# Attention, routing and two expert layers on one core: wider units of q and k, and an earlier place for the store of a group's rows

## The chip, the cores and the metric

The kernel runs on one core of a Trainium2 chip (trn2). The core has five engines that run their own instruction queues: TensorE (PE; its weight loads are shown apart as PEld), VectorE (DVE), ScalarE (ACT), GpSimd (POOL) and SyncE (SP, which here only issues DMAs). The metric is the device time of one execution, in microseconds (us); times of kernels are medians of several executions, and one further execution of each was recorded by the hardware profiler.

## The reference

```python
# q, k, v: [8 batches, 8 heads, 576 tokens, 64]; attention within chunks of 64 tokens
scores = (q_c @ k_c.T) / 8;  attn = softmax(scores);  x = (attn @ v_c) as [4608 tokens, 512]

# first expert layer: tokens with x @ w_skip > 0 go to one of 8 experts
e = argmax(x @ w_gate);  g = softmax(x @ w_gate)[e]
x[chosen] += g * (relu(x @ w1[e]) @ w2[e])          # w1 512x1024, w2 1024x512

# second layer, dense
h = max(relu(x @ w1'), x @ w2', x @ w3');  out = h @ w_out   # 512x768, 768x512
```

All of it is in 32-bit floats. The large products are made of three products of split operands (a high and a low part).

## The kernel before

The kernel has three stages. The first, the only one that the diff touches, makes attention and routing for 36 tiles of 128 tokens; the second runs the experts over gathered rows; the third is the dense layer in blocks of 1024 tokens.

**The loop of the first stage** (line 578) has one step t for each tile, and a tile passes through it over several steps. In step t: `cross(t)` (line 210) copies halves of the tile's v to the other 64 partitions (POOL, tile vm, four buffers); `pair_heads` (218) regroups q and k of a later unit (POOL, tiles qr and kr, three buffers); `values(t - 2)` (278) multiplies attention by v and writes the rows xg (DVE, line 300); `load_v` brings v of tile t + 6; `scores(t)` (244) makes q k, maximum, difference and exponential; `exp_transpose(t - 1)`; `logits(t - 3)`; `qk_transpose` (226) turns regrouped q and k, 4 transposes each on PE (tiles trq, trk, line 237), and ACT copies them out (line 239); `x_transpose(t - 2)` turns the rows (trx, line 313). PE's order is the written one (`manual_schedule`, 577). The other engines' queues are ordered by the scheduler of the build, from the written order and its own estimate of times, so an instruction may stand ahead of its written place or behind it.

**Units.** q and k come in 18 units of 256 tokens (UT). A partition holds two consecutive tokens (r=2), so for each head a packet of a load is 2 x 64 floats, 512 bytes. `load_qk` (190) issues q and k on SP, in two pieces each where a unit lies in two batches; five units have buffers (tags b4, s4, b8 of bpool), and a unit's load waits until the regroup of the fifth unit before has read the buffer. Unit u + 1 is turned in steps 2u and 2u + 1, four heads in each. The turned tiles qT and kT are 4 x 256 per partition with two buffers.

**Groups.** Routing runs over groups of four tiles (the last two groups have two). The step after a group's last logits has `route(g)` (324): some 20 small DVE instructions and an exponential; one of them, the reciprocal at line 343, writes the gate weight into the group's rows xg. A step later `place(g)` (378) makes ranks and slots, and `store_x(g)` (445) stores the group's rows to DRAM, 1 MB, issued by POOL. The rows of a group have two buffers (bpool tag xg), so the first rows of group g + 2 wait for the store of group g. `send_id(t - 9)` (425) scatters the 128 token numbers of a tile to their slots in DRAM, an indirect DMA issued by POOL. After group 5, the ids come back from DRAM, and DVE and POOL prepare the first gathers of the experts (lines 630 to 638).

From step 22 on, weights of expert 0 are loaded and split in even steps into wpool (tag w, 16 buffers of 4 KB per partition, two for each of eight pieces).

Of the kernel before, what the change touches and what calls it, by code (L numbers as in the profile page):

```python
# [28 lines left out]
NU = N // UT  # L29
# [8 lines left out]
def kernel(  # L38
# [151 lines left out]
    def load_qk(u):  # L190
        if u % 5 < 3:
            qt = four_kb([P, H, 2 * D], F32, f"qt{u}", u % 5 == 2)
            kt = four_kb([P, H, 2 * D], F32, f"kt{u}", u % 5 == 2)
        else:
            both = bpool.tile([P, 2, H, 2 * D], F32, tag="b8", name=f"qkt{u}")
            qt, kt = both[:, 0], both[:, 1]
        for h0, h1 in [(0, 4), (4, 8)] if u == 0 else [(0, 8)]:
            for off, b, s, n in pieces(u * UT, (u + 1) * UT):
                pr = slice(off // 2, (off + n) // 2)
                for dst, src in ((qt, q), (kt, k)):  # L200
                    link["load"] = nc.sync.dma_start(
                        dst[pr, h0:h1], src[b, h0:h1, s:s + n, :].rearrange("h (p r) d -> p h (r d)", r=2))
        units[u] = {"qt": qt, "kt": kt}
# [14 lines left out]
    def pair_heads(u, g):  # L218
        un = units[u]
        for nm in ("q", "k"):  # L220
            r = apool.tile([P, 2, H // 2, D], F32, tag=nm + "r", name=f"{nm}r{u}_{g}", bufs=3)
            (nc.scalar.copy if u == 0 else nc.gpsimd.tensor_copy if u > 1 else nc.vector.tensor_copy)(
                r, un[nm + "t"][:, 4 * g:4 * g + 4, :].rearrange("p h (r d) -> p r h d", r=2))
            un[nm + "r", g] = r

    def qk_transpose(u, g):
        un = units[u]
        if g == 0:
            for nm in ("qT", "kT"):
                un[nm] = apool.tile([P, 4, UT], F32, tag=nm, name=f"{nm}{u}")  # L230
        for nm in ("q", "k"):
            src, dst = un[nm + "r", g], un[nm + "T"]
            tr = ps_tr(f"tr{nm}{u}_{g}").rearrange("p (h r t) -> p h r t", h=2, r=2)
            for hh in range(2):
                hp = 2 * g + hh
# [3 lines left out]
            (nc.vector.tensor_copy if nm == "k" and u == 0 else nc.scalar.copy)(  # L239
                dst[:, 2 * g:2 * g + 2, :].rearrange("p h (t r) -> p h r t", r=2), tr)  # L240
# [3 lines left out]
    def scores(t):  # L244
        u, s = divmod(t, 2)
        un = units[u]
# [316 lines left out]
    for u in range(5):  # L563
# [5 lines left out]
        if u < 2:  # L569
            pair_heads(u, 0)  # L570
            pair_heads(u, 1)
            if u == 0:
                qk_transpose(0, 0)
                qk_transpose(0, 1)
# [555 lines left out]
```

## Time and profile before

| | |
|---|---|
| three runs | 1135.57, 1136.97, 1143.81 us; median 1136.97 |
| profiled execution | 1130.38 us; span from first to last instruction 1128.7; mean granted clock 0.952 |
| PE | 1032.5 us busy, 91% of the span |
| DVE, ACT, POOL | 570.0, 418.7, 363.8 us busy |
| loads of q and k, 512 KB | median 7.0 and 7.3 us from issue to landing (tiles qt, kt) |
| stores of a group's rows, 1040 KB | median 6.7 us |

How to read the rows: an engine's busy time is what its instructions fill; its waits are idle stretches, put down to the event that came last among those that the instruction waited for. Where a wait is for several events and one is an engine that updates all the time, the name shown can be that engine's though another event ended the wait. [...] A DMA share of 1.00 means that 16 engines' worth of packet time was used. A tile's name stands without its number.

### The profile page before, as it was taken

The page shows a single profiled execution, that of the slowest core. Times are in us where ns is not written, and L with a number is a line of the kernel's source. Part 1 is how long each engine was busy: PE and PEld are TensorE (multiplying, and loading weights), DVE is VectorE, ACT ScalarE, POOL GpSimd, SP SyncE. Part 2 cuts the span into 40 slices and gives each one's busy share as a digit, 9 for nine tenths or more (in the row PEclk, how much of TensorE's full clock was granted, in tenths as well). Part 3 has the DMA queues.
Part 4 walks back from the last instruction along what each step waited for, and adds up shares of the span by engine and source line. Part 5 has one row for each costly group of instructions (what it writes and reads, how often), then busy time and mean ns, then how long its engine had stood idle before and what let it go on. Part 6 is the DMA issues. An engine that isn't in the chain of part 4 may idle for free.

```text
span 1128.7 us, 19653 instructions
## 1 busy us (share of the span) xinstructions
PE 1032.5 (91%) x7544; PEld 879.0 (78%) x7544; DVE 570.0 (51%) x1118; ACT 418.7 (37%) x737; POOL 363.8 (32%) x411
## 2 busy tenths in 40 slices
PE   8967886897999997999899799999999999999997
PEld 6866875795887886888688588778887788788896
DVE  4653664646973646542479781444334352343241
ACT  5644554533543433451434352222322242222231
POOL 3445566344451335350332241111311140122121
PEclk9988788798999998999999899999999999999999
DMA  9999754446783728461998835665456644666590
GB/s 211 231 261 213 181 156 148 152 142 226 246 284 111 264 91 281 165 221 47 286 327 297 274 105 182 179 182 154 166 158 188 195 131 142 193 195 199 180 294 37
DMA packets 213105, 217.12 MB, mean 192 GB/s; under 512 B 48267, under 2 KB 177291, under 8 KB 212992
## 3 DMA queue, kind: packets, MB, share of 16 engines
q1 hardware_dynamic: 199808, 174.18, 53.2%
q0 software_dynamic: 10592, 33.20, 8.6%
q10 hardware_dynamic: 2592, 8.26, 1.9%
q8 instruction: 69, 1.13, 0.4%
q14 instruction: 44, 0.36, 0.1%
HBM read 175.15 MB, written 41.83 MB: 192 GB/s over the span
## 4 chain that ended last, share of the span: by engine, by line
PE 44%; DMA 5%; DVE 1%; issue 0%; ACT 0%; SPq 0%; ACTq 0%; DVEq 0%
PE f_a L687 6%; PE f_a L689 6%; PE f_a L688 6%; PE o L687 4%; PE o L689 4%; PE o L688 4%; DMA ws<-m_sums 4%; PE f_d L687 3%; PE f_d L688 3%; PE f_d L689 3%; PE f_b L689 1%; PE f_b L688 1%; PE f_b L687 1%; PE trf L861 1%; DMA m_sums<-n_q 1%
## 5 line engine op out<-in xcount | busy, mean ns | idle before, releaser
L91 POOL TENSOR_TENSOR fh<-best,fh 128x512 fp32r<-128x512 f32 (+1 forms) x60 | 77.0, 1288 | 360.3 <-ACT fh L90 276.1
L687 PE MATMUL f_a<-x_t,ws 128*128 128x512 f32 (+1 forms) x270 | 100.9, 374 | 6.8 <-DVE p L1015 5.5
L688 PE MATMUL f_a<-x_t,ws 128*128 128x512 f32 (+1 forms) x270 | 99.9, 370 | 0.0
L689 PE MATMUL f_a<-x_t,ws 128*128 128x512 f32 (+1 forms) x270 | 99.7, 370 | 0.0
L90 ACT CAST whi_e<-raw_e 128x1024 fp32r<-128x1024 f32 x64 | 65.9, 1048 | 65.2 <-DMA raw_e<-in_moe_w_dram 33.8
L687 PE MATMUL h<-xhi,whi_e 128*128 128x256 f32 x256 | 74.6, 292 | 13.2 <-ACTq L964 7.4
L688 PE MATMUL o<-wlo_m,fh 128*128 128x512 f32 x216 | 84.6, 392 | 0.0
L687 PE MATMUL o<-whi_m,fh 128*128 128x512 f32 x216 | 83.4, 392 | 0.0
L689 PE MATMUL o<-whi_m,fh 128*128 128x512 f32 x216 | 83.4, 392 | 0.0
L688 PE MATMUL h<-xlo,whi_e 128*128 128x256 f32 x256 | 73.8, 289 | 0.1
L687 PE MATMUL y<-whi_e,hhi 128*128 128x512 f32 x184 | 73.2, 400 | 0.6 <-ACT hhi L754 0.6
L689 PE MATMUL h<-xhi,wlo_e 128*128 128x256 f32 x256 | 73.4, 288 | 0.0
L689 PE MATMUL y<-whi_e,hlo 128*128 128x512 f32 x184 | 72.2, 396 | 0.2
L688 PE MATMUL y<-wlo_e,hhi 128*128 128x512 f32 x184 | 71.8, 392 | 0.0
L91 POOL TENSOR_TENSOR wlo_e<-raw_e,whi_e 128x1024 fp32r<-128x1024 f32 x21 | 52.8, 2516 | 51.2 <-ACT whi_e L90 50.9
L90 ACT CAST fh<-best 128x512 fp32r<-128x512 f32 (+1 forms) x60 | 34.8, 579 | 90.7 <-DVE best L1017 59.0
L91 DVE TENSOR_TENSOR wlo_e<-raw_e,whi_e 128x1024 fp32r<-128x1024 f32 x43 | 55.8, 1313 | 23.4 <-ACT whi_e L90 21.4
L687 PEld LDWEIGHTS f_a<-x_t,ws 128*128 128x128 f32 x270 | 51.1, 189 | 16.5 <-DVE p L1015 5.9
L687 PEld LDWEIGHTS h<-xhi,whi_e 128*128 128x128 f32 x256 | 50.4, 197 | 16.1 <-ACTq L964 10.8
L1020 ACT COPY p<-f_a 128x512 f32<-128x512 f32 (+1 forms) x45 | 24.6, 546 | 97.8 <-PE f_a L689 95.0
L678 POOL DMA_INDIRECT x_dram<-xg,ids_sb x20 | 20.8, 1039 | 115.3 <-DVEq L902 46.9
L689 PEld LDWEIGHTS f_a<-x_t,ws 128*128 128x128 f32 x270 | 51.2, 190 | 8.6
(220 smaller groups left out, 2709.5 us busy)
## 6 DMA issues: line engine op xcount, KB each, us to landing
ws<-m_sums SPq DMA_DIRECT2D x135, 512.0 KB, 5.0
raw_e<-in_moe_w_dram SPq DMA_DIRECT2D x64, 512.0 KB, 4.5
ws<-m_sums SPq DMA_DIRECT2D x45, 256.0 KB, 3.9
x<-x_dram SPq DMA_DIRECT2D x36, 256.0 KB, 4.9
out_dram<-os SPq DMA_DIRECT2D x36, 256.0 KB, 2.2
x_dram<-xg POOLq DMA_DIRECT2D x8, 1040.0 KB, 6.7
v_all<-in_v_dram SPq DMA_DIRECT2D x32, 256.0 KB, 6.9
m_sums<-n_raw ACTq DMA_DIRECT2D x18, 448.0 KB, 4.6
```

What stands on the lines that cost most here:

```text
L90: nc.scalar.copy(hi, src),
L91: eng.tensor_tensor(lo, src, hi.bitcast(F32), op=ALU.subtract),
L678: ins = nc.gpsimd.indirect_dma_start(out=x_dram[:, :], out_offset=bass.IndirectOffsetOnAxis(ap=ids, axis=0), in_=xg, in_offset=None, bound ...
L687: nc.tensor.matmul(acc, ahi, bhi, start=first, stop=False, skip_group_check=onto)
L688: nc.tensor.matmul(acc, ahi, blo, start=False, stop=False, skip_group_check=onto)
L689: return nc.tensor.matmul(acc, alo, bhi, start=False, stop=last, skip_group_check=onto)
L861: nc.tensor.transpose(tr[:, i * P:(i + 1) * P], row[:, c * P:(c + 1) * P], ident)
L1020: nc.scalar.copy(p1, acc_a)
```

## The change

q and k keep two units of 256 tokens and then go on in eight units of 512. In a wide unit a partition holds four consecutive tokens, so a packet is 4 x 64 floats, 1 KB. A load item of a wide unit is four heads of all 512 tokens (512 KB of q and as much of k, as before), so a wide unit has two items (`item_of`); an item is regrouped and turned in two jobs of two heads' pairs each. The jobs have a list of steps of their own: up to step 3 two at a time, then job t + 6 is regrouped and job t + 4 turned in step t (before: t + 4 and t + 2). An item's load is written in the step after its buffer's last regroup. Turned tiles of even units lie in qT and kT, now of 4 x 512 with one buffer; those of odd units take wpool buffers, one each for q and k of unit 1 and two each for the others. `unit_of` tells in which unit a tile lies, and `scores` reads from there. ACT's copies of wide units write every fourth element, where they wrote every second one.

`store_x(g)` moves from behind `place(g)` to behind `route(g)`, one step earlier.

```diff
--- before.py
+++ after.py
@@ -26,7 +26,8 @@
 F2 = 768
 KC = DM // P
 UT = 256
-NU = N // UT
+NI = N // UT
+WIDE = 2
 NT = N // P
 XW = DM + 8
 COLS = NT
@@ -187,20 +188,33 @@
             t += n
         return got
 
-    def load_qk(u):
-        if u % 5 < 3:
-            qt = four_kb([P, H, 2 * D], F32, f"qt{u}", u % 5 == 2)
-            kt = four_kb([P, H, 2 * D], F32, f"kt{u}", u % 5 == 2)
+    def unit_of(t):
+        return divmod(t, 2) if t < 2 * WIDE else (WIDE + (t - 2 * WIDE) // 4, t % 4)
+
+    def item_of(i):
+        return (i, None) if i < WIDE else (WIDE + (i - WIDE) // 2, i % 2)
+
+    def load_qk(i):
+        if i % 5 < 3:
+            qt = four_kb([P, 1024], F32, f"qt{i}", i % 5 == 2)
+            kt = four_kb([P, 1024], F32, f"kt{i}", i % 5 == 2)
         else:
-            both = bpool.tile([P, 2, H, 2 * D], F32, tag="b8", name=f"qkt{u}")
+            both = bpool.tile([P, 2, 1024], F32, tag="b8", name=f"qkt{i}")
             qt, kt = both[:, 0], both[:, 1]
-        for h0, h1 in [(0, 4), (4, 8)] if u == 0 else [(0, 8)]:
-            for off, b, s, n in pieces(u * UT, (u + 1) * UT):
-                pr = slice(off // 2, (off + n) // 2)
+        U, g = item_of(i)
+        if g is None:
+            r, t0, heads = 2, i * UT, [(0, 4), (4, 8)] if i == 0 else [(0, 8)]
+        else:
+            r, t0, heads = 4, WIDE * UT + (U - WIDE) * 2 * UT, [(4 * g, 4 * g + 4)]
+        for h0, h1 in heads:
+            for off, b, s, n in pieces(t0, t0 + P * r):
+                pr = slice(off // r, (off + n) // r)
                 for dst, src in ((qt, q), (kt, k)):
+                    to = dst[pr].rearrange("p (h x) -> p h x", x=r * D)
                     link["load"] = nc.sync.dma_start(
-                        dst[pr, h0:h1], src[b, h0:h1, s:s + n, :].rearrange("h (p r) d -> p h (r d)", r=2))
-        units[u] = {"qt": qt, "kt": kt}
+                        to[:, h0:h1] if g is None else to,
+                        src[b, h0:h1, s:s + n, :].rearrange("h (p r) d -> p h (r d)", r=r))
+        units[i] = {"qt": qt, "kt": kt}
 
     def load_v(t):
         for off, b, s, n in pieces(t * P, (t + 1) * P):
@@ -215,42 +229,54 @@
             to, of = slice(64 * par, 64 * par + 64), slice(64 - 64 * par, 128 - 64 * par)
             eng.tensor_copy(vm[t][to], vn[of, par])
 
-    def pair_heads(u, g):
-        un = units[u]
+    def pair_heads(job):
+        i, x = divmod(job, 2)
         for nm in ("q", "k"):
-            r = apool.tile([P, 2, H // 2, D], F32, tag=nm + "r", name=f"{nm}r{u}_{g}", bufs=3)
-            (nc.scalar.copy if u == 0 else nc.gpsimd.tensor_copy if u > 1 else nc.vector.tensor_copy)(
-                r, un[nm + "t"][:, 4 * g:4 * g + 4, :].rearrange("p h (r d) -> p r h d", r=2))
-            un[nm + "r", g] = r
-
-    def qk_transpose(u, g):
-        un = units[u]
-        if g == 0:
-            for nm in ("qT", "kT"):
-                un[nm] = apool.tile([P, 4, UT], F32, tag=nm, name=f"{nm}{u}")
+            r = apool.tile([P, 2, H // 2, D], F32, tag=nm + "r", name=f"{nm}r{job}", bufs=3)
+            raw = units[i][nm + "t"]
+            part = (raw.rearrange("p (h r d) -> p r h d", h=H, r=2)[:, :, 4 * x:4 * x + 4, :] if i < WIDE else
+                    raw.rearrange("p (h r d) -> p r h d", h=4, r=4)[:, 2 * x:2 * x + 2])
+            (nc.scalar.copy if i == 0 else nc.gpsimd.tensor_copy if i > 1 else nc.vector.tensor_copy)(r, part)
+            units[nm, job] = r
+
+    def qk_transpose(job):
+        i, x = divmod(job, 2)
+        U, g = item_of(i)
+        w = UT if i < WIDE else 2 * UT
+        if U not in turned:
+            turned[U] = {}
+            for nm in ("q", "k"):
+                if U % 2:
+                    halves = 1 if U < WIDE else 2
+                    made = [wpool.tile([P, 4 // halves, w], F32, tag="w", name=f"{nm}T{U}_{n}") for n in range(halves)]
+                else:
+                    both = apool.tile([P, 4, 2 * UT], F32, tag=nm + "T", name=f"{nm}T{U}", bufs=1)
+                    made = [both[:, 2 * n:2 * n + 2, :w] for n in range(2)]
+                turned[U][nm] = [m[:, n:n + 2] for m in made for n in range(0, m.shape[1], 2)]
         for nm in ("q", "k"):
-            src, dst = un[nm + "r", g], un[nm + "T"]
-            tr = ps_tr(f"tr{nm}{u}_{g}").rearrange("p (h r t) -> p h r t", h=2, r=2)
+            src = units[nm, job]
+            dst = turned[U][nm][x if i < WIDE else g].rearrange("p h (t r) -> p h r t", t=P)
+            tr = ps_tr(f"tr{nm}{job}").rearrange("p (h r t) -> p h r t", h=2, r=2)
             for hh in range(2):
-                hp = 2 * g + hh
                 for r in range(2):
                     nc.tensor.transpose(
                         tr[:, hh, r, :], src[:, r, 2 * hh:2 * hh + 2, :].rearrange("p h d -> p (h d)"), ident)
-            (nc.vector.tensor_copy if nm == "k" and u == 0 else nc.scalar.copy)(
-                dst[:, 2 * g:2 * g + 2, :].rearrange("p h (t r) -> p h r t", r=2), tr)
+            (nc.vector.tensor_copy if nm == "k" and i == 0 else nc.scalar.copy)(
+                dst if i < WIDE else dst[:, :, 2 * x:2 * x + 2], tr)
 
     TILES = [(par, c2) for par in range(2) for c2 in range(2)]
 
     def scores(t):
         u, s = divmod(t, 2)
         un = units[u]
+        U, at = unit_of(t)
         sc = two_banks("sc", f"sc{t}")[:, :, :4 * 64].rearrange("p r (h k) -> p r h k", h=4)
         for hp in range(4):
             for par, c2 in TILES:
                 rows, cols = slice(64 * par, 64 * par + 64), slice(64 * c2, 64 * c2 + 64)
-                toks = slice(64 * (2 * s + c2), 64 * (2 * s + c2) + 64)
+                toks = slice(64 * (2 * at + c2), 64 * (2 * at + c2) + 64)
                 nc.tensor.matmul(
-                    sc[cols, par, hp, :], un["qT"][rows, hp, toks], un["kT"][rows, hp, toks],
+                    sc[cols, par, hp, :], *[turned[U][nm][hp // 2][rows, hp % 2, toks] for nm in ("q", "k")],
                     start=True, stop=True)
         mx = apool.tile([P, 2, 4], F32, tag="mx", name=f"mx{t}")
         link["max"] = nc.vector.reduce_max(mx, sc, axis=AX)
@@ -548,7 +574,7 @@
 
     AHEAD = 11
 
-    vm, units, xt, groups, slots, picks, xgs, xT, link, put, sent = {}, {}, {}, {}, {}, {}, {}, {}, {}, {}, []
+    vm, turned, units, xt, groups, slots, picks, xgs, xT, link, put, sent = {}, {}, {}, {}, {}, {}, {}, {}, {}, {}, {}, []
     ids_rows = ids_dram.rearrange("(p c) o -> p (c o)", p=P)
 
     def in_turn(load, *what):
@@ -567,22 +593,29 @@
         if u == 2:
             in_turn(load_gates)
         if u < 2:
-            pair_heads(u, 0)
-            pair_heads(u, 1)
+            pair_heads(2 * u)
+            pair_heads(2 * u + 1)
             if u == 0:
-                qk_transpose(0, 0)
-                qk_transpose(0, 1)
+                qk_transpose(0)
+                qk_transpose(1)
+    regroups = [(4,), (5, 6), (7, 8), (9,)]
+    turns_at = [(2,), (3,), (4, 5), (6, 7)]
+    regroups += [(t + 6,) for t in range(4, NT - 6)]
+    turns_at += [(t + 4,) for t in range(4, NT - 4)]
+    items = list(range(5, NI))
+    regrouped = 1
     LAG, late, raws_0 = GT + 5, range(NT - 2), {}
     in_order = ExitStack()
     in_order.enter_context(tc.manual_schedule(engines={mybir.EngineType.PE}))
     for t in range(NT + LAG):
         u, s = divmod(t, 2)
-        if s == 0 and u + 5 < NU:
-            load_qk(u + 5)
+        while items and items[0] - 5 <= regrouped:
+            load_qk(items.pop(0))
         if t < NT:
             cross(t)
-        if u + 2 < NU:
-            pair_heads(u + 2, s)
+        for job in regroups[t] if t < len(regroups) else ():
+            pair_heads(job)
+            regrouped = (job - 1) // 2
         if t == 8:
             nc.gpsimd.tensor_copy(tok_f, tok_i)
             nc.gpsimd.tensor_scalar_add(tok_f, tok_f, float(-N))
@@ -606,21 +639,21 @@
             exp_transpose(t - 1)
         if 0 <= t - 3 < NT:
             logits(t - 3)
-        if u + 1 < NU:
-            qk_transpose(u + 1, s)
+        for job in turns_at[t] if t < len(turns_at) else ():
+            qk_transpose(job)
         if 0 <= t - 2 < NT:
             x_transpose(t - 2)
         if 0 <= t - 3 < NT:
             g, j = PLACE[t - 3]
             if j + 1 == SIZES[g]:
                 route(g)
+                store_x(g)
         if 0 <= t - 4 < NT:
             g, j = PLACE[t - 4]
             if j + 1 == SIZES[g]:
                 if g == 2:
                     count_first()
                 place(g)
-                store_x(g)
                 if g == FIRST or START[g] + SIZES[g] == DIRECT:
                     for i in range(max(late[0], t - LAG), START[g + 1]):
                         send_id(i)
```

## Rows read from the trace of the kernel before

**Rows 1.** The page, part 2: granted clock and DMA share in 40 slices of 28 us.
```profile
...
PEclk9988788798999998999999899999999999999999
DMA  9999754446783728461998835665456644666590
...
```

**Rows 2.** Windows; columns: length, each engine's busy us (instructions), PEclk, DMA share, GB/s.
```profile
...
56.00:96.00 40.00, 27.05 (x460) 24.44 (x460) 19.44 (x66) 17.20 (x37) 18.92 (x33) 0.81 1.05 239
96.00:145.00 49.00, 40.33 (x735) 36.84 (x737) 25.60 (x88) 24.71 (x52) 24.64 (x43) 0.81 0.81 198
145.00:215.00 70.00, 54.70 (x1033) 48.21 (x1025) 41.70 (x128) 37.14 (x75) 40.12 (x70) 0.85 0.44 137
...
112.00:122.00 10.00, 8.33 (x98) 7.78 (x102) 5.58 (x23) 4.77 (x10) 5.88 (x10) 0.50 0.61 128
...
```

**Rows 3.** PE's waits in 56 to 96, then in 96 to 215: us, times, longest.
```profile
...
PE trq L237 <- POOL qr L222: 10.1, 3, 4.3
PE trx L313 <- DVE rpr L345: 1.5, 1, 1.5
...
PE trx L313 <- DVE xg L300: 12.9, 3, 6.9
PE trx L313 <- DVE rmx L333: 1.9, 1, 1.9
...
PE trk L237 <- POOL kr L222: 1.1, 1, 1.1
...
PE trq L237 <- POOL qr L222: 0.6, 2, 0.3
...
```

**Rows 4.** The waits of VectorE (DVE) in 50 to 215.
```profile
...
DVE xg L300 <- DMA x_dram<-xg: 14.9, 5, 4.4
DVE at L636 <- DMA ids<-ids_dram: 9.6, 1, 9.6
...
```

**Rows 5.** Groups of POOL in 56 to 210: busy, mean ns | idle before, releasers.
```profile
...
L427 POOL DMA_INDIRECT ids_dram<-tok_i,rslot x28 | 27.7, 989 | 6.8 <-issue 4.2 <-POOL vm L216 1.1 <-DVE xg L300 0.7
L216 POOL COPY vm<-v_all 64x260 f32<-64x260 f32 x52 | 21.2, 408 | 60.7 <-DMA ids_dram<-tok_i,rslot 29.9 <-PE trx L313 8.4 <-PE xp L285 5.8
...
L449 POOL DMA_DIRECT2D x_dram<-xg x6 | 4.9, 810 | 0.0
...
```

**Rows 6.** POOL's timeline: start, length, instruction [idle before, releaser].
```profile
...
74.16 0.81 POOL L449 DMA_DIRECT2D x_dram<-xg  x1
...
108.03 0.98 POOL L427 DMA_INDIRECT ids_dram<-tok_i,rslot  x1 [0.30 <-issue]
114.23 0.85 POOL L216 COPY vm<-v_all 64x260 f32<-64x260 f32 x2 [5.22 <-DMA ids_dram<-tok_i,rslot]
...
118.60 0.98 POOL L427 DMA_INDIRECT ids_dram<-tok_i,rslot  x1 [0.16 <-POOL vm L216]
...
126.09 0.84 POOL L216 COPY vm<-v_all 64x260 f32<-64x260 f32 x2 [5.31 <-PE trx L313]
...
```

**Rows 7.** DMA queues and issues in 0 to 40, in 80 to 130, and in 700 to 760.
```profile
...
q1 hardware_dynamic: 21423, 8.14, 103.7%
...
ids_dram<-tok_i,rslot POOLq DMA_INDIRECT x8, 5.5
...
q1 hardware_dynamic: 12755, 11.09, 63.7%
...
```

**Rows 8.** VectorE's timeline: second group's route, and first rows of the fourth.
```profile
...
57.02 0.19 DVE L333 TENSOR_REDUCE rmx<-lg 128x4 f32<-128x32 f32 x1
...
59.60 0.17 DVE L343 RECIPROCAL xg<-rsm 128x4 f32<-128x4 f32 x1
...
81.65 0.69 DVE L300 TENSOR_TENSOR xg<-xp,sm 128x512 f32<-128x512 f32 x1 [3.87 <-DMA x_dram<-xg]
...
```

**Rows 9.** Groups in 0 to 220: transposes of q, and ScalarE's copies of them.
```profile
...
L237 PE MATMUL trq<-ident,qr 128*128 128x128 f32 x144 | 27.0, 318 | 11.3 <-POOL qr L222 10.7 <-ACT qr L222 0.4
...
L239 ACT COPY qT<-trq 128x512 f32<-128x512 f32 x36 | 22.2, 621 | 10.9 <-PE trq L237 10.6
...
```

## The prediction

> **What bounds it now.** I read the page's 40 slices first, then the stage windows, then PE's waits in them, and then the queue of the engine that PE waits for. The slices of 28 us show the granted clock at nine tenths or more from the eleventh on, but for two; the slack is in the eight slices before 226 us, the attention and routing stage, where the clock's digits fall to 8 and 7 and DMA is at nine tenths for the first four [rows 1]. By windows, PE is busy 27.05 of 40 us in 56 to 96, 40.33 of 49 in 96 to 145 and 54.70 of 70 in 145 to 215, at mean clocks of 0.81, 0.81 and 0.85 [rows 2]. [...]
>
> Who makes PE wait changes at 96. Before it, PE waits 10.1 us in 3 waits for POOL's regrouped q (trq from qr). After it, POOL costs only 0.6 and 1.1 us; the transposes of attention rows cost 12.9 us in 3 waits (trx from xg) and 1.9 more [rows 3]. What VectorE waits for there is split into two kinds: xg waits 14.9 us in 5 pieces for the store of the rows that last held its buffer, and once 9.6 us for the ids that come back from DRAM [rows 4]. The longest of PE's three trx waits, 6.9 us, is over any wait for a store (4.4 at most), so I take it for the second kind, which the change leaves. So the store's share of PE's waiting is 1.5 + 1.9 + (12.9 - 6.9) = 9.4 us at most, of which 1.5 lies before 96.
>
> POOL looks idle and isn't free. From 56 to 215 its instructions fill 18.92 + 24.64 + 40.12 = 83.7 of 159 us [rows 2], and up to 210 the copies vm wait 60.7 us; the sends, next in idle time, wait 6.8 [rows 5]. So nothing but the vm waits holds it. The view puts 29.9 us of them on the scatter of the ids and the rest on several PE groups [rows 5], but the timeline shows one pattern: a send of ids at 108.03, then the next vm at 114.23; a send at 118.60, the next vm at 126.09 [rows 6]. That is 6.2 and 7.5 us, about the 5.5 us median landing of such a send in this stretch plus the send itself [rows 7]. I take all these waits as landings. There are nine of over 2 us by 145, four of them by 96. Then POOL is a chain of its own, copy, send, landing, copy, as fast as a scatter lands beside 1 MB bursts of q and k, and PE is held by POOL first and by the store's landing later.
>
> **The change, part by part.**
>
> Packets. A unit of 512 tokens turns two 512-byte packets into one of 1 KB, 16 items of 1 MB (q and k together), and leaves the first two units alone. No row shows 512 bytes alone. In the first 40 us q1 used 103.7% of 16 engines for 21423 packets and 8.14 MB: 0.0310 us each at 380 bytes on average. In 700 to 760, where ws is read in pieces of 1 KB and some of 512 bytes, it used 63.7% for 12755 packets and 11.09 MB: 0.0479 us each at 869 bytes [rows 7]. A 512-byte packet so lies between 31 ns (size without effect) and 42 (time by bytes), one of 1 KB between 48 and 56. Two less one saves 6 to 36 ns; but the late stretch is calmer, so the low end is zero. An item is 64 packets of 1 KB on each engine: 0 to 2.3 us. I take 1.0, nearer the low end because the early row may owe its price to the crowd and not to the size.
>
> What that is worth: each of the nine long vm waits lies behind such a burst. The four by 96 at 1.0 us each are 4 us, against 10.1 us that PE waits for POOL there: **-4** (0 to -9.2). The five from 96 to 145 make POOL 9 us earlier by then, which the next part needs. After 145 no q or k is loaded and nothing more is won.
>
> [...]
>
> The store. It moves from behind place(g) to behind route(g), one loop step earlier. It needs only route's reciprocal. For the second group the route ran from 57.02 to 59.77, with the reciprocal at 59.60, the store was issued at 74.16, and the fourth group's first rows waited for its buffer until 81.65 [rows 6, 8]. A step is about 6 us (36 in some 215), and the longest wait is 4.4 [rows 4]: all five go. Of PE's 9.4 us the 1.5 before 96 would be taken up by the wait for POOL; the other 7.9 lie on PE's path. What is late next is POOL's regrouped q; POOL is 9 us earlier by the part above, so I count the whole: **-7.9** (0 if POOL is not earlier). On POOL it moves past a send, a vm pair and a pair of regroup copies; SP's queue does not hold it. It takes 0.81 us at its new place as now [rows 5]; behind it wait vm and the regroup copies, which PE needs two steps later.
>
> The clock. In 112 to 122, right after such a stall, the granted clock was 0.50 with 8.33 us busy [rows 2]: at the upper level that is 4.2 us less. Over 56 to 145 a mean of 0.81 means 34 us at the lower level, three quarters of them busy: at most 13 us to win back. I take **-2**, since other waits (ids, ACT) stay and can lower it too.
>
> Order of the turns. Transposes of q and k now run up to two jobs further ahead. 144 transposes of q take 27.0 us busy, so a job of 4 for q and 4 for k is 1.5 us, two are 3.0 [rows 9]: later at the front, where the first 512-token unit needs two items in place of one before its scores, and missing at the tail. Bounds +3 to -3, taken **-1**, as the front has idle engines and the tail has none. ScalarE writes with twice the stride; qT takes 621 ns now [rows 9], and even 60 ns more on 64 copies is 4 us on an engine under half busy: 0. SP issues 14 DMAs more (66 for 52): 0, up to 7 us early on if each costs half a us. The odd units take four slots in wpool, where expert pieces claim two per even step from 24 on; by count 14 of 16 at step 28: 0.
>
> Sum: -4 - 7.9 - 2 - 1 = -15. The profiled execution, 1130.4 us with 1128.7 of span and 1.7 around it, would be 1115.4; the median of the three runs is 1137.0, 6.6 above it, and the same gain makes that 1122. What follows the stage is bound by PE and moves with it.
>
> **Rivals.**
>
> A, small gain. The packets win nothing or the scheduler keeps the store where it was on POOL (it orders POOL by its own estimate, not by the source): POOL's chain stands, PE runs into it and keeps about half of the 7.9, and 1 of order: -5, 1132. For it: POOL has no spare time at all between 56 and 210 [rows 5]. Against it: PE waits for POOL only 1.7 us after 96 [rows 3].
>
> B, all waits fall together. 10.1 + 9.4 and the 13 of the clock: -32, 1105. For it: a stall costs twice, as idle and as lower clock after it [rows 2]. Against it: the landing would have to fall by several us.
>
> C, slower. The store now stands on POOL right behind route, and POOL waits there in order for VectorE's reciprocal, with vm and the regroup copies queued behind. POOL is the pacing chain, so it pays in full: six stores between 56 and 210 [rows 5] at up to the 2.75 us of a route [rows 8] are 16.5, less the 9 of the shorter landings: +7.5, 1144.5. It decides once POOL reaches the store before L343 is done. For it: POOL loses time nowhere else in-between. Against it: today POOL reaches the store 14.6 us after the reciprocal [rows 6, 8].
>
> **Numbers.** Forecast 0.5, A 0.25, B 0.12, C 0.13. The forecast's own range is 1113 to 1130. Into the range of 8 in 10 go nearly all of B and A and most of C: 1102 to 1143. One per cent, 11.4 us, is about what a measurement of this kernel tells from no change. Faster by more: B, and three quarters of the forecast: 0.5. Slower by more: that part of C in which a worse front comes on top, and what none of the four names: 0.12. Within: 0.38.
>
> **What would show it.** Right: no wait of xg for the store in VectorE's waits; the stores on POOL's timeline some 10 us closer behind route; vm waits in 56 to 145 shorter by about a us each; q1 with some 16000 packets fewer; the last scores some 13 to 16 us earlier; PEclk digits of the first slices higher. Wrong: a gap on POOL before L449 (C); the vm waits as long as now and PE's waits moved from trx to trq (A); a wait for item 3 or 5 before the scores of the first wide units (the front).

## The result, and the profile after

The changed kernel took 1153.59 us (median of 4, 1151.86 to 1154.56), the kernel before, run beside it, 1136.27: a ratio of 1.014, 95% interval 1.0097 to 1.0182, 17 us slower. On another chip the medians were 1149.15 and 1129.97 us. Of the ten executions of the changed kernel there two count as slow and are left out of the ratio, which is again 1.0141. Medians of one kernel differ between chips by up to 7 us, so each run below is given as its ratio to the kernel before on the same chip (formed from the single runs; the quotient of two medians, 1.015 for the first pair, can differ a little). The profiled execution is 1151.86 us with a span of 1150.1, against 1130.38 and 1128.7.

The page's slices, to be held against [rows 1]: four slices of DMA at nine tenths as there, the fifth at 8 instead of 7, and the clock's digits before 226 us are no better. (PEclk is the granted clock as a share of TensorE's full speed. In the kernel before it stood at 1.00 in 42 of the 80 stretches of 2 us from 56 to 216 us and at 0.50 in 22; the other 16 lie in between, none below.)

```profile
...
PEclk9978797669899999899999989999999999999999
DMA  9999845236676446753699854665456645666591
...
```

The windows that answer to [rows 2]. PE is busy longer in 56 to 96 and 145 to 215 and shorter in 96 to 145: no stage is won.

```profile
...
56.00:96.00 40.00, 30.41 (x541) 26.97 (x542) 17.66 (x52) 22.11 (x38) 15.45 (x27) 0.83 1.20 232
96.00:145.00 49.00, 37.61 (x586) 32.92 (x586) 21.96 (x75) 24.92 (x43) 28.01 (x47) 0.76 0.85 193
145.00:215.00 70.00, 57.85 (x1003) 51.77 (x1002) 43.77 (x135) 44.60 (x75) 35.95 (x61) 0.83 0.46 142
...
```

PE's waits in 56 to 96, then in 96 to 215, for [rows 3]. The two that the prediction counted on shrank, from 10.1 to 4.3 us and from 12.9 to 4.3.

```profile
...
PE trq L262 <- POOL qr L239: 4.3, 2, 3.9
...
```

```profile
...
PE trx L339 <- DVE xg L326: 4.3, 2, 2.9
...
```

DVE's waits in 50 to 215, for [rows 4], and then POOL's in 56 to 215. The wait for the store fell from 14.9 to 1.6 us on DVE and stands on POOL instead, with 37.9 us, where the next group's pad columns are cleared.

```profile
...
DVE at L669 <- DMA ids<-ids_dram: 7.5, 1, 7.5
...
DVE xg L326 <- DMA x_dram<-xg: 1.6, 2, 1.0
...
```

```profile
...
POOL xg L322 <- DMA x_dram<-xg: 37.9, 7, 8.6
POOL vm L230 <- DMA ids_dram<-tok_i,rslot: 20.5, 6, 6.7
...
POOL x_dram L475 <- DVE run L383: 2.5, 2, 1.5
...
```

POOL's timeline there, for [rows 6]: store, memset, and then the four sends of ids that stood one in each step before.

```profile
...
83.90 0.82 POOL L475 DMA_DIRECT2D x_dram<-xg  x1
...
93.45 0.12 POOL L322 MEMSET xg<- 128x28 f32 x1 [7.15 <-DMA x_dram<-xg]
...
94.29 1.02 POOL L453 DMA_INDIRECT ids_dram<-tok_i,rslot  x1 [0.16 <-DVE xg L326]
95.62 0.98 POOL L453 DMA_INDIRECT ids_dram<-tok_i,rslot  x1 [0.30 <-issue]
...
```

So the waits that the forecast named became shorter, and the kernel became slower. Where the time is lost shows only in the progress of the tiles. The table gives the start of VectorE's maximum (tile mx) of tiles 8, 14, 20 and 35 (the first is 0; 35 is the last), from DVE's timeline; "again" are second profiles of the same two kernels.

| first maximum of tile | 8 | 14 | 20 | 35 |
|---|---|---|---|---|
| before, before again | 45.8, 46.8 | 82.3, 81.8 | 124.1, 124.7 | 216.1, 218.7 |
| after, after again | 54.2, 54.0 | 94.1, 96.5 | 137.0, 134.4 | 232.5, 228.9 |

Seven to eight us are lost by tile 8 and 12 to 15 by tile 14; from there the distance is 10 to 16. In those stretches the load queue (q1) has changed. Its rows in 0 to 40 and in 50 to 90 us (packets, MB, share of 16 engines):

```profile
...
q1 hardware_dynamic: 17876, 8.36, 103.3%
...
```

```profile
...
q1 hardware_dynamic: 12899, 7.24, 107.3%
...
```

In the first 40 us a full queue moved 8.36 MB, hardly more than before [rows 7]: packets of 1 KB won next to nothing. In 50 to 90 it is over-full with 7.24 MB, where the kernel before moved 8.37 MB at 95.0%.

ScalarE's copies, for [rows 9]: 621 ns became 1042 on average, about 1.1 us for a wide unit.

```profile
...
L264 ACT COPY kT<-trk 128x512 f32<-128x512 f32 x34 | 37.8, 1111 | 0.9 <-PE trk L262 0.9
L264 ACT COPY qT<-trq 128x512 f32<-128x512 f32 x36 | 37.4, 1042 | 13.6 <-PE trq L262 13.3 <-issue 0.2
...
```

### The profile page after: what moved, and what is told of

It is laid out like the page before. It is cut to its first block, busy times and chain, and to the rows that moved or that the text cites. A ratio compares the mean times of both kernels' runs of the same rounds, so it can differ in the third digit from the quotient of the medians.

```text
span 1150.1 us, 19676 instructions
## 1 busy us (share of the span) xinstructions
PE 1050.0 (91%) x7544; PEld 890.4 (77%) x7544; DVE 576.3 (50%) x1118; ACT 440.8 (38%) x737; POOL 369.1 (32%) x411
## 4 chain that ended last, share of the span: by engine, by line
PE 39%; DMA 6%; DVE 3%; issue 2%; POOL 1%; ACT 0%; SPq 0%; POOLq 0%; DVEq 0%; ACTq 0%
PE f_a L720 5%; PE f_a L722 5%; PE f_a L721 5%; PE o L720 4%; PE o L722 4%; PE o L721 4%; DMA ws<-m_sums 3%; PE f_d L720 3%; PE f_d L722 2%; PE f_d L721 2%; DMA m_sums<-n_q 2%; PE f_b L720 1%; PE f_b L722 1%; PE f_b L721 1%; PE trf L894 1%
```

## The experiments

The theories, as they came up. S: ScalarE's stride of 16 bytes. O and Q: GpSimd's queue, with the memset waiting for the store. F: the front, two more jobs and one more load item before the first wide scores. P: the packet's size. D: loads in pieces. A unit of 512 tokens crosses the end of a batch (576 tokens) in 7 of 8 cases, so 14 of the 16 wide items come in two pieces of 16 to 112 partitions each; of the 18 narrow units 6 do. U: the wide units by themselves. W: the wide loads or the stride. N: the number of DMAs. R: another order of the dense layer.

| run | ratio to before, 95% | tile 14 | tile 35 |
|---|---|---|---|
| after_again | 1.0141 (1.0100 to 1.0182) | 96.5 | 228.9 |
| e1_pairs | 1.0090 (1.0059 to 1.0121) | 96.1 | 233.0 |
| e2_store_back | 1.0101 (1.0062 to 1.0139) | 96.2 | 231.3 |
| e3_store_only | 0.9934 (0.9907 to 0.9962) | 82.2 | 215.6 |
| e4_stride | 1.0008 (0.9981 to 1.0036) | 82.2 | 223.9 |
| e7_pool_order | 1.0328 (1.0285 to 1.0371) | 92.5 | 251.0 |
| e8_lead | 1.0027 (1.0002 to 1.0052) | 88.0 | 217.6 |
| e9_512 | 1.0118 (1.0077 to 1.0159) | 96.2 | 234.8 |
| e10_store_but4 | 0.9989 (0.9958 to 1.0021) | 80.2 | 217.8 |
| e11_store_4 | 0.9934 (0.9899 to 0.9969) | 84.4 | 214.8 |
| e12_one_piece | 0.9983 (0.9960 to 1.0006) | 82.0 | 212.1 |
| e13_two_pieces | 1.0080 (1.0047 to 1.0113) | 95.4 | 229.2 |
| e14_late | 0.9973 (0.9949 to 0.9997) | 98.8 | 216.9 |
| e15_order | 0.9977 (0.9947 to 1.0007) | 81.1 | 214.5 |
| e16_order_narrow | 0.9918 (0.9887 to 0.9950) | 72.1 | 202.9 |
| e17_order_pairs | 0.9953 (0.9924 to 0.9981) | 79.8 | 208.4 |
| e18_two_whole | 0.9985 (0.9962 to 1.0007) | 94.0 | 218.4 |

**The stride: e1_pairs and e4_stride.**

```diff
 e1_pairs, on the changed kernel
-                dst if i < WIDE else dst[:, :, 2 * x:2 * x + 2], tr)
 ...
+                nc.scalar.copy(
+                    dst[:, :, 2 * x:2 * x + 2].rearrange("p h r t -> p h t r"), tr.rearrange("p h r t -> p h t r"))
 e4_stride, on the kernel before
-                un[nm] = apool.tile([P, 4, UT], F32, tag=nm, name=f"{nm}{u}")
+            both = apool.tile([P, 4, UT, 2], F32, tag="qkT", name=f"qkT{u}")
+            for n, nm in enumerate(("qT", "kT")):
+                un[nm] = both[:, :, :, n]
```

> The changed kernel, with the elements of ScalarE's copies of wide q and k in another order: it writes the two tokens that lie side by side one after the other (8 bytes, then 8 bytes further on), instead of 128 elements each 16 bytes apart and then the next row. All queues keep their order. Theory S (the stride): the copies go from 1.04 and 1.11 us back to 0.6 to 0.75 us, ScalarE's busy time falls by 20 to 32 us, and most of the loss of 17 us goes: 1135 to 1144 us. Theory O (order: the store's wait moved to GpSimd's memset of pad columns, two more jobs of transposes ahead of the first wide scores): the copies get shorter, but the time stays at 1149 to 1154 us.

> The kernel before with q and k turned into one tile in which they alternate, so that ScalarE's copies write elements 16 bytes apart instead of 8, on the narrow units; loads, store, jobs and the order of every queue stay. The scores read with a stride of 8 bytes; should that cost TensorE anything, the rows of the scores show it. Theory S: the copies take 1.0 to 1.15 us instead of 0.62, ScalarE is 30 to 36 us busier, and the time is 1147 to 1156 us. Theory O: 1136 to 1140 us.

The groups of ScalarE's copies in e1_pairs, then in e4_stride:

```profile
...
L267 ACT COPY kT<-trk 128x512 f32<-128x512 f32 x32 | 20.1, 629 | 3.8 <-PE trk L262 3.5 <-issue 0.2
L267 ACT COPY qT<-trq 128x512 f32<-128x512 f32 x32 | 20.0, 625 | 11.2 <-PE trq L262 11.0
...
```

```profile
...
L240 ACT COPY qkT<-trq 128x512 f32<-128x512 f32 x36 | 39.0, 1089 | 11.6 <-PE trq L238 11.5 <-issue 0.2
L240 ACT COPY qkT<-trk 128x512 f32<-128x512 f32 x34 | 38.5, 1133 | 0.0
...
```

The copies went to 0.63 us in the one and to 1.1 us in the other, as theory S had it, but the times didn't follow. e1_pairs stands at 1.0090, and e2_store_back, which is the changed kernel's order on the same chip, at 1.0101; tile 35 comes when that of the changed kernel does. 34 us more of ScalarE's copies in the kernel before made it 0.1% longer (interval -0.2 to 0.4%), though its profiled execution, 1138.89 us, has tile 35 five to eight us late. Theory S falls as the main cause. The stride itself is real: 0.59 us for a copy of the same size that writes without gaps (aT), 0.62 at 8 bytes, 1.1 at 16.

**The store: e2_store_back, e3_store_only, e10_store_but4, e11_store_4.**

```diff
 e2_store_back, on the changed kernel (e3_store_only: the reverse, on the kernel before)
                 route(g)
-                store_x(g)
 ...
                 place(g)
+                store_x(g)
 e10_store_but4 (e11_store_4: g == 4), on the kernel before
                 route(g)
+                if g != 4:
+                    store_x(g)
 ...
                 place(g)
-                store_x(g)
+                if not (g != 4):
+                    store_x(g)
```

> The changed kernel with the store written behind place(g) again. In the queues built from it every instruction stands where it stood in the changed kernel. Both theories then expect no change, 1151 to 1156 us: the written place of the store decides nothing once the units are wide, and the store's place that the trace shows belongs to the other half of the change. A gain of over 5 us would mean that something outside the order of the queues was changed with it.

> The kernel before with only the store moved behind route(g). Forecast's own step: VectorE's waits of xg for the store (14.9 us) go and the time falls by up to 7.9 us, to 1128 to 1132. Theory O: the store comes a few us earlier on GpSimd, but GpSimd's memset of the next group's pad columns moves up with it and waits for it there: 1139 to 1147 us. Theory S says nothing against either; if it explains the whole loss, this part alone is worth 0 to -8: 1129 to 1138 us.

e2_store_back is the changed kernel's queues word for word, and its tiles' times are the changed kernel's: the new written place of the store did nothing there. (The ratios of these two, 1.0101 and 1.0141, lie 0.4% apart, which shows what two sets of runs can differ by.) e3_store_only hit the forecast's number, 7.5 us, and looked like a proof of it. It isn't. Its tiles come no earlier, and DVE still waits 11.1 us for the store, of 14.9 [rows 4]:

```profile
...
DVE xg L300 <- DMA x_dram<-xg: 11.1, 3, 6.5
...
```

The gain lies in the dense layer, in the first block. The rows of the first output product (tile o; first start behind the comma) of before, e3, e10 and e11, in this order:

```profile
...
L687 PE MATMUL o<-whi_m,fh x216: 387/389/481, 652.3 to 1120.4; 128*128 128x512 f32 x108
...
```

```profile
...
L687 PE MATMUL o<-whi_m,fh x216: 387/389/478, 645.6 to 1114.9; 128*128 128x512 f32 x108
...
```

```profile
...
L690 PE MATMUL o<-whi_m,fh x216: 387/389/481, 657.8 to 1126.7; 128*128 128x512 f32 x108
...
```

```profile
...
L690 PE MATMUL o<-whi_m,fh x216: 387/389/476, 648.2 to 1117.6; 128*128 128x512 f32 x108
...
```

The first product of the layer starts at 546.4, 548.0, 552.7 and 548.8, so the block takes 105.9, 97.6, 105.1 and 99.4 us; in the second profile of the kernel before it takes 102.0 (550.7 to 652.7). The scheduler of the build orders TensorE's queue in the dense layer, and moving the store of one group in the first stage tipped it into another order of the first block's transposes and products. e10 and e11 were made to tell this from the store.

> The kernel before with the store written behind route for all groups but the fifth (group 4). GpSimd's queue differs from before only around group 1, and TensorE's order in the dense layer is that of before, which in the kernel with all stores moved is another. Theory R (the gain of the store alone, 0.66%, came from the other order in the dense layer and not from the store): 0.998 to 1.002 of before. The forecast's step (VectorE's wait for the store lies on TensorE's path): 0.993 to 0.997.

> The kernel before with the store of group 4 alone written behind route. One store moves by one place or two on GpSimd, and the dense layer gets the other order. Theory R: 0.992 to 0.996, the dense layer's first block (first product to first output) 96 to 99 us instead of 102 to 106, the attention stage as before. The forecast's step: one store of five, 0.998 to 1.000.

All stores but that of group 4 written earlier: 0.9989. That of group 4 alone: 0.9934. So the gain goes with the other order of the dense layer: by the profiles the block is 3 to 8 us shorter in e3 and e11, and their last tiles come half a us to 4 us earlier. The earlier written place by itself gave nothing that can be measured. In e10's queue, though, GpSimd's order differs only around group 1, so what five stores that do come earlier would be worth, no run here shows. The changed kernel has the old order in the dense layer.

**GpSimd's queue and the job list: e7_pool_order, e8_lead, and the two kernels again.**

```diff
 e7_pool_order, on the changed kernel
-    in_order.enter_context(tc.manual_schedule(engines={mybir.EngineType.PE}))
+    in_order.enter_context(tc.manual_schedule(engines={mybir.EngineType.PE, mybir.EngineType.Pool}))
 e8_lead, on the changed kernel
-WIDE = 2
+WIDE = NI
```

> The changed kernel once more, beside the next three. All theories: within 0.5% of its first time, 1147 to 1157 us; its last tile's maximum again some 15 to 18 us later than in the kernel before.

> The kernel before once more, for a second profile: how far two executions of one kernel differ in each stage. Expected: the last tile's maximum within 3 us of 216.1, the end within 8 us of 1128.7.

> The changed kernel with GpSimd's queue in the written order during the attention stage: the pad memset of a group stands at its first values, one send of ids in each step, the store right after route. Units, jobs, loads and strides stay. Theory Q (the queue order that the scheduler made for the new job list puts the memset, which waits for the store, and four sends in a row ahead of vm, qr and kr): GpSimd's 37.9 us of memset waits go, TensorE gains 6 to 12 us, 1136 to 1144 us. Theory F (the front: item 3 and two more jobs must be done before the scores of tile 4): stays within 3 us of the changed kernel.

> The changed kernel with narrow units throughout (512-byte packets, 256 tokens, ScalarE's stride of 8 bytes), but with the job list of the change, two jobs further ahead than before. Its queue on GpSimd has the memset right behind the store as in the changed kernel. Theories Q and F (both come from the job list): as slow as the changed kernel, 1146 to 1154 us, the maximum of tile 8 at 53 to 58 us. Theory W (the wide loads or the stride cost it): back at 1136 to 1140 us, tile 8 at 46 to 49 us.

The written order on GpSimd was worse by another 1.9%: there is one send in each step, and the vm copies behind them held TensorE. TensorE's waits in 56 to 230:

```profile
...
PE xp L311 <- POOL vm L230: 23.1, 12, 4.5
...
```

So this run doesn't decide on theory Q. e8_lead does: the memset waits nearly as long there as in the changed kernel, and the kernel is only 0.27% slower than before. POOL's waits in 56 to 215:

```profile
...
POOL xg L322 <- DMA x_dram<-xg: 32.1, 7, 5.9
...
```

The job list costs 10 us by tile 8 (55.7) and 6 by tile 14, but 1.5 by tile 35: what it takes at the front comes back later. Theories Q and F fall as the main cause, and theory W, the wide loads, remains. (e8, e13 and e18 share a third order of the dense layer's first block, 101.9 to 102.6 us, and are best compared with each other; all other runs but e3 and e11 have the order of before.)

**Packet, pieces or units: e9_512, e12_one_piece, e13_two_pieces, e14_late, e18_two_whole.**

```diff
 e9_512, on the changed kernel
-                    link["load"] = nc.sync.dma_start(
 ...
+                    of = src[b, h0:h1, s:s + n, :].rearrange("h (p a r) d -> p h a (r d)", a=r // 2, r=2)
+                    for a in range(r // 2):
+                        link["load"] = nc.sync.dma_start(
+                            to[:, h0:h1, a] if g is None else to[:, :, a], of[:, :, a])
 e12_one_piece, on the changed kernel
-            for off, b, s, n in pieces(t0, t0 + P * r):
+            for off, b, s, n in pieces(t0, t0 + P * r) if g is None else [(0, t0 // S, min(t0 % S, S - P * r), P * r)]:
 e13_two_pieces, on e8_lead, from unit 2 on
+        if len(got) == 1:
+            off, b, s, n = got[0]
+            got = [(0, b, s, n // 8), (n // 8, b, s + n // 8, n - n // 8)]
 e18_two_whole, on e8_lead
+            heads = [(0, 4), (4, 8)] if i == 0 or i > 1 and len(pieces(t0, t0 + UT)) == 1 else [(0, 8)]
 e14_late, on the changed kernel
-WIDE = 2
+WIDE = 6
 ...
+    w = 2 * WIDE
 ...
+    regroups += [(t + 6,) for t in range(w, NT - 6)]
+    turns_at += [(t + 4,) for t in range(w, NT - 4)]
```

> The changed kernel with each load of a wide item in two DMAs of 512-byte packets (tokens 0 and 1 of a partition, then 2 and 3) over the same partitions and heads; units, job list and TensorE's order stay. In the changed kernel from 50 to 90 us a packet of 1 KB took 82 ns, 1 KB of 512-byte packets in the narrow kernel with the same job list 62 ns. Theory P (the size of the packets costs it): 512-byte packets take 31 to 35 ns there, the load queue's share falls, tile 20 comes at 126 to 130 us instead of 134 to 137, and the time is 1.000 to 1.006 of before. Theory U (the wide units themselves: what must be loaded and turned before a tile's scores): stays at 1.011 to 1.018.

The load queue of e9_512 in 50 to 90 us:

```profile
...
q1 hardware_dynamic: 18300, 7.15, 109.8%
...
```

By the trace's packet records its 512-byte packets took 46 ns there, not 31 to 35. The loads came no faster than the changed kernel's 7.24 MB, and neither did the tiles. Theory P falls.

> The changed kernel, where each load of a wide item reads 512 tokens that lie in one batch (q and k of other tokens than the reference's where a unit crosses a batch's end), so that each is one DMA over all 128 partitions; before, 14 of 16 items lie in two batches and come in two pieces each, of 16 to 112 partitions. Bytes, packet size and all queues but SP's stay. Theory D (DMAs over part of the partitions slow the loads): packets of 1 KB in 50 to 90 us take 60 to 70 ns instead of 82, tile 14 comes at 86 to 91 us instead of 94 to 96, and the time is 1.002 to 1.008 of before. Theory U (the wide units themselves, whatever the pieces): tile 14 at 93 to 97 us, 1.010 to 1.016.

> The narrow kernel with the job list of the change (1.0027 of before), each of its q and k loads from unit 2 on split in two DMAs of 16 and 112 partitions where it lies in one batch. Order of the engines' queues as there, but for one step of two copies on GpSimd. Theory D: loses what the wide kernel loses, tile 14 at 92 to 96 us instead of 88, 1.008 to 1.014 of before. Theory U: 1.001 to 1.005, tile 14 at 87 to 90 us.

> The narrow kernel with the job list of the change, each q and k load from unit 2 on that lies in one batch split in two by heads (4 and 4), so that there are as many DMAs as in e13, but each over all 128 partitions. Theory D (part of the partitions): as the kernel without the split, 1.000 to 1.005 of before, 512-byte packets in 65 to 80 us at 29 to 34 ns, tile 14 at 86 to 90 us. Theory N (the number of DMAs, issued and finished one after the other): as e13, 1.006 to 1.011, 44 to 46 ns, tile 14 at 93 to 97 us.

> The changed kernel with six narrow units ahead of the wide ones instead of two (12 tiles instead of 4), and the job list two jobs ahead only from step 10 on. Theory F2 (the loss is the front's 7 us, the two jobs and the item more that must be there before the first wide scores, and the crowded loads behind it): tile 8 back at 46 to 48 us, and the time 1.002 to 1.008 of before. Theory U (each wide unit costs): 5 of 8 wide units are left (6 of 16 items gone), so 1.007 to 1.011.

The load queue of e12_one_piece in 0 to 40 and 50 to 90 us:

```profile
...
q1 hardware_dynamic: 20129, 9.97, 99.4%
...
```

```profile
...
q1 hardware_dynamic: 13124, 6.85, 70.7%
...
```

In pieces, 8.36 MB passed in the first 40 us; whole, 9.97, with the queue as full. By the trace's packet records from 20 to 50 us a packet of 1 KB took 78 ns on average in the changed kernel and 52 here. All engines but SP work in the order of the changed kernel. The whole loss is gone, 1.0141 to 0.9983, and tile 14 comes at 82.0 instead of 94 to 97.

From the other side, the queue in 50 to 90 us of e8_lead, of e13_two_pieces and of e18_two_whole, which splits as many loads, but by heads, so that each DMA goes to all partitions:

```profile
...
q1 hardware_dynamic: 21136, 8.26, 85.7%
...
```

```profile
...
q1 hardware_dynamic: 19198, 7.49, 109.2%
...
```

```profile
...
q1 hardware_dynamic: 21722, 8.25, 93.9%
...
```

Split by partitions, 109.2% for 7.49 MB; split by heads, 93.9% for 8.25. In time: 1.008 and 0.9985, tile 35 at 229.2 and 218.4. So it is not the number of DMAs; what slows the queue is that a DMA goes to part of the partitions. The price is smaller than in the changed kernel: e13 loses 0.5% on e8_lead. (e18's tile 14 came at 94.0, later than expected; at tile 20 it is 2 us behind e8_lead, 128.2 against 126.4.)

The kernel before shows the same within one run. Its q and k loads are the only 512-byte packets in the queue in the first 200 us, 2048 to a unit. In order of start, the packets of units 2, 4, 6, 11, 13 and 15, which lie in two batches, took 39 to 50 ns on average, those of the other twelve 28 to 36. Units 4 and 13 are cut into halves of 64 partitions and took 49.5 and 45.3, so unequal pieces are not what it takes. In the changed kernel the 14 items in pieces took 62 to 90 ns a packet and the two whole ones, the last, 50 and 47. What in a DMA over part of the partitions makes its packets longer, no trace here shows.

e14_late is explained only in part. It has six wide units left, not the five that its expectation counted, and ten of their twelve items are in pieces. Its load queue in 50 to 90 us moves no more than the changed kernel's 7.24 MB:

```profile
...
q1 hardware_dynamic: 14550, 7.19, 97.2%
...
```

At tile 14 it is the latest of all (98.8); then it makes tiles 20 to 30 in 54 us, where the kernel before takes 63, and ends level with that kernel. So loads in pieces don't cost the same in every order of the work. Six of these eight us may be VectorE's one wait for the ids, 9.6 us in [rows 4]; its row in 100 to 240 here:

```profile
...
DVE at L670 <- DMA ids<-ids_dram: 3.7, 1, 3.7
...
```

What shortened it was not tried. GpSimd's queue has a third order there, in which the memset waits 3.1 us for the store in 56 to 215 and not 37.9; whether that wait costs something where loads come in pieces is open too.

**Whole loads with the reference's result: e15_order, e16_order_narrow, e17_order_pairs.** Another order of the tokens, the first 512 of each batch and then the last 64 of all, keeps every unit but the last ones in one batch.

```diff
-            b, s = divmod(t, S)
-            n = min(end - t, S - s)
+            b, s = divmod(t, 512) if t < 512 * B else divmod(t - 512 * B, S - 512)
+            s, n = (s, min(end - t, 512 - s)) if t < 512 * B else (s + 512, min(end - t, S - 512 - s))
 ...
-                nc.sync.dma_start(out[r:r + P, :], o)
+                for off, bb, s, m in pieces(r, r + P):
+                    nc.sync.dma_start(out[bb * S + s:bb * S + s + m, :], o[off:off + m])
```

> The changed kernel with another order of the tokens: the first 512 of each batch make eight units' worth of tiles, the last 64 of the eight batches the remaining four tiles, and the rows go out in the reference's order. Now only the last unit of q and k lies in several batches. Theory D: as the run with one piece each, 0.994 to 1.002 of before, tile 14 at 80 to 84 us, 1 KB packets at 50 to 56 ns until the last unit. Theory U: 1.010 to 1.016.

> The kernel before with that order of the tokens: narrow units, none in two batches but the last two, store where it was, ScalarE's stride of 8 bytes. Tells what the order alone is worth from what wide units add to it. If whole loads are all that counts: as e15, 0.990 to 1.000. If the 1 KB packets count too: 0.3 to 1% above e15.

> e15 with ScalarE's copies of q and k written in pairs, 0.63 us instead of 1.1. With the loads out of the way ScalarE's 32 us may come onto the path: theory S2, 3 to 8 us below e15. Otherwise within 2 us of it.

e15_order repeats e12_one_piece with the reference's tokens: 0.9977. e16_order_narrow, the kernel before with that order of the tokens, is the fastest of all, 0.9918, and beats both kernels: its last tile comes 13 us earlier, and the ratio is worth 9 us. Neither of its two expectations had it below e15. The build also gave GpSimd, VectorE and ScalarE another order (the sends stand four in a row there, as in the changed kernel), so how much of the 9 us the loads alone are worth isn't shown. Its load queue in 0 to 40 us:

```profile
...
q1 hardware_dynamic: 24112, 9.48, 99.8%
...
```

That is 9.48 MB against the 8.14 of [rows 7]: the kernel before has 6 units in two batches, two of them in the first five, and paid for them too. The change as a whole adds nothing on top: e15 lies above e16, with the list's late front (tile 8 at 52.6 against 45.0) and a longer wait for the ids (14.5 against 6.8 us). What wide units would give without that list was not run. e17 is below e15 by 0.24%, with intervals that overlap: the stride may cost 3 us once the loads are fast, which isn't shown.

## Why the prediction was wrong

**Packets, -4 (0 to -9.2).** This is the step that failed, and with it the sign. The estimate of 48 to 56 ns for a packet of 1 KB was right for a load over all partitions (52 ns); in two pieces it was 78 on average in 20 to 50 us, as long as two of 512 bytes before (39 each, in part cut themselves; 30 where they are whole, in e16), and 82 in 50 to 90, where the kernel before took 33 for 512 bytes. The prediction had seen that there are more DMAs and wrote "SP issues 14 DMAs more (66 for 52): 0". It priced their number (by the traces 66 for 50, so 16 more) and didn't ask what the additional ones are: pieces over part of the partitions. The lower bound of zero was wrong as well, since nothing excluded a loss. "No row shows 512 bytes alone" was true of the rows, but the packet records of the kernel before had both prices, 28 to 36 ns for whole units and 39 to 50 for cut ones. What the pieces cost the changed kernel is about 18 us: 1.0141 less 0.9977 (e15) or 0.9983 (e12), of 1130. That it need not cost so much in another order of the work, e14_late shows.

With whole loads 1 KB moved 19.6 bytes per ns (e15, 20 to 50 us) and 512 bytes 16.8 (e16), so in these runs size does count, once the loads are whole.

**Store, -7.9.** "It moves ... one loop step earlier", "all five go": it did not move. The queue of GpSimd is the scheduler's, and the written place shifted two stores in the narrow kernel and none in the wide one. Rival A had the mechanism (the scheduler keeps the store where it was) and a price on the wrong side of zero. DVE's waits did go in the changed kernel (14.9 to 1.6 us), but because POOL's memset now waits first, and nothing was won by it. e8_lead, where the memset waits 32.1 us, stands at 1.0027.

**Clock, -2.** The mean of the span did not rise: 0.944 for 0.952. Executions of the kernel before alone lie between 0.940 and 0.962, so that is no clear fall either.

**Order of the turns, -1 (+3 to -3).** At tile 8 the list costs 10 us (e8_lead), not 3: the forecast counted the 3.0 us of transposes and no wait for the loads they need, though they stand in TensorE's written order ahead of the scores. Three of the ten are there at tile 4 (31.5 for 28.5); behind it TensorE waits 3.6 us, to 35.8, for the regrouped q of the fifth item, whose load GpSimd awaits. What makes the rest is open. At the end 0.27% is left, about 3 us.

**ScalarE, 0.** The size was wrong by a factor of eight, some 480 ns (1.1 us less 0.62) instead of "even 60 ns more", the verdict right: 0.1% (e4_stride).

**Rivals.** C, with a chance of 0.13, gave the right side, and its 1144.5 came nearest to the 1153.59; that is luck, for its reason is wrong: GpSimd waits 2.5 us at the stores for VectorE in 56 to 215, not 16.5. The "wait for item 3 or 5 before the scores of the first wide units" stood among the signs to look for and had no price.

## What to carry to other kernels

When a change makes tiles or units of another size, list what its DMAs become, boundary by boundary: a transfer that is cut at a boundary of the data so that it covers part of the partitions can cost more than the larger packet wins (here about 18 us of 1130), for everything else in the queue too (packets of 256 bytes at 34 ns instead of 21). Where a scheduler orders the queues, read the built order before pricing a line that was moved. And when an experiment gives the predicted number, look in which stage it was won: most of the 7.5 us that stood where 7.9 were forecast came from another layer.

## What was not expected of the hardware

DMAs over part of the partitions lower the rate of a full load queue: 7.81 to 8.36 MB in the first 40 us with pieces (e13, after), 9.5 to 10.1 without (e16, e12, e15). Other loads in the queue slow down with them: in 50 to 90 us packets of 256 bytes took 34 ns in the changed kernel and 21 in e15, 29 in e13 and 21 in e8. ScalarE's write of single 4-byte elements 16 bytes apart takes nearly twice as long (1.1 us) as one 8 bytes apart (0.62), and in pairs at the same distance it is as fast as that (0.63).
